# Probability buffers as fixed tiles taken in turn, with the writes of one buffer declared ordered, in a one-core adaLN attention and Mish MLP block

## The chip, the cores and the metric

The kernel runs on one core of a Trainium2 chip, alone. The metric is the device time of one launch in microseconds (us), the median over several runs. Before the change it is 1747.98 us, the median of three runs (1747.57, 1747.98 and 1752.33).

The core has five engines that each take their instructions strictly in order: PE (TensorE, matrix products), ACT (ScalarE, exponentials and copies), DVE (VectorE, maxima and sums), POOL (GpSimd) and SP (which issues the transfers). They meet only through semaphores: an instruction may wait until a counter of another engine, or of its own, has reached a value.

## The reference, cut to what matters

```python
B, S, D = 1, 2048, 512
H = 32; Dh = D // H                 # 32 heads of 16
scale = Dh ** -0.5
scores = jnp.einsum("bhqd,bhkd->bhqk", q, k) * scale
p = _softmax(scores, axis=-1)
o = jnp.einsum("bhqk,bhkd->bhqd", p, v)
...
x = x + ga * _A_ref(h, A_wqkv, A_wo)                  # h: layer norm of x, scaled and shifted
x = x + gb * _B_ref(h, B_w1, B_b1, B_w2)              # dense, Mish, dense; F = 1792
```

All inputs and the output are 32-bit floats. The softmax runs over 2048 keys for each of 2048 queries and 32 heads, so 32 x 2048 x 2048 exponentials are taken; these are the "probabilities".

## The kernel before, in words

**Tiling.** The queries are cut into 4 blocks of 512 and the heads into 8 groups of 4, which gives 32 iterations `n`. An iteration goes over the 2048 keys in 16 chunks of 128, so there are 512 steps `t` (`t = 16 n + chunk`), recorded one after the other by `step`. In each step four score products are made (`score`, the matmul of line 507: 64 rows of the array, 512 queries wide), each is exponentiated by ACT (line 510, `nc.scalar.activation(pr, p_, AF.Exp, ...)`) into a probability buffer `pr`, and four products of probabilities with values follow two steps later (`pv`, line 525, output `bk`, input `vg` and `pr`). Beside that, each step makes four products for the row maxima of a later iteration (`max_tile`, line 470), which DVE reduces (line 472), and a part of other work: projections, output projection and MLP of the query block before (line 132).

**Buffers.** Scores and maxima share a ring of six PSUM banks (`ring`). A score product can start when the exponential or the maximum that used its bank six turns ago has been read out. The probabilities go into SBUF tiles of 128 x 512 floats: four tags `p0` to `p3`, one for each head of the group, with 3 buffers for the heads of the lower half of the rows (`s = 0`) and 4 for the upper half (`s = 1`), 14 buffers in all. The pool hands them out: `ap.tile([P, TB], F32, tag=f"p{2 * j + s}", name="pr", bufs=3 + s)`. The pool `ap` is made with `reuse_waits="tile"`. The tail of the kernel takes eight tiles of the same tags for the last query block (`y` and `xn`).

**Order.** Nothing is reordered by a scheduler: the kernel is recorded under `manual_schedule`, so each engine's order is that of the code. What the recording layer adds are the waits. An exponential into a buffer that was used before must not start before the values' product has read the old contents (a wait on PE, which it needs for its scores anyway) and, in the layer's view, must also come after the older exponential that wrote that buffer (a wait of ACT on its own counter). Where one instruction has to wait for two counters, the first wait stands in a separate EVENT_SEMAPHORE instruction ahead of it in the same queue.

Of the kernel before, what the change touches and what calls it, by code (L numbers as in the profile page):

```python
# [8 lines left out]
F32 = mybir.dt.float32  # L9
# [9 lines left out]
def adaln_block(ctx: ExitStack, tc: tile.TileContext, x, wqkv, wo, w1, b1, w2, c, w_mod, out):  # L19
    nc = tc.nc  # L20
    P = 128
    S, D = x.shape[1], x.shape[2]
# [5 lines left out]
    TB = 512  # L28
# [4 lines left out]
    T = 16 * NIT  # L33
# [66 lines left out]
    def layernorm(pool, xt, xn, eng="v"):  # L100
        st = pool.tile([P, 6], F32, tag="ln_st", name="ln_st", bufs=4)
        mv = pool.tile([P, 2], F32, tag="ln_mv", name="ln_mv", bufs=4)
        rs = pool.tile([P, 2], F32, tag="ln_rs", name="ln_rs", bufs=4)
        nc.vector.bn_stats(out=st, in_=xt)
        nc.vector.bn_aggr(out=mv, in_=st)
        nc.gpsimd.tensor_scalar(rs[:, 0:1], mv[:, 1:2], 1.0, EPS, op0=ALU.mult, op1=ALU.add)
        nc.gpsimd.tensor_tensor(rs[:, 1:2], rs[:, 0:1], nhalf, op=ALU.pow)
        eng = nc.vector if eng == "v" else nc.gpsimd
        return lambda: eng.tensor_scalar(xn, xt, mv[:, 0:1], rs[:, 1:2], op0=ALU.subtract, op1=ALU.mult)
# [28 lines left out]
    def pe_run():  # L138
        while pe_queue:
            mm_go(pe_queue.pop(0))  # L140
# [6 lines left out]
    def ring(w=1):  # L147
        if w == 2 and ring_at[0] % 2:
            ring_at[0] += 1
        b = ring_at[0] % NRING  # L150
        ring_at[0] += w
        return ring_t[:, b, :] if w == 1 else ring_t[:, b:b + 2, :]

    def bank(tag="ms"):
        return ring() if tag == "ring" else ps.tile([P, TB], F32, tag=tag, name="bk", bufs=1)
# [153 lines left out]
    with ExitStack() as es:  # L309
# [28 lines left out]
        e = lp.tile([P, DK], F32, name="sil_e")  # L338
# [39 lines left out]
        pr, pm = [], ring()[:, :2 * DK].rearrange("p (i k) -> p i k", k=DK)  # L378
# [72 lines left out]
    ap = ctx.enter_context(tc.tile_pool(name="ap", bufs=1, reuse_waits="tile"))  # L451
# [46 lines left out]
                        mt[o:o + 8, :].bitcast(F32))  # L498
        at(2 * (16 * n + 16 - PRO) + 3, put)

    pts = {}

    def score(n, j, s, kc):
        def product():
            kt, qt = ka[(2 * n + j) % NR], qa[(2 * n + j) % NR]
            p_ = ring()
            nc.tensor.matmul(p_, kt[64 * s:64 * s + 64, kc * P:(kc + 1) * P], qt[64 * s:64 * s + 64, :],  # L507
                             start=True, stop=True)
            pr = ap.tile([P, TB], F32, tag=f"p{2 * j + s}", name="pr", bufs=3 + s)
            e = nc.scalar.activation(pr, p_, AF.Exp, scale=SCALE)  # L510
            pts[16 * n + kc, 2 * j + s] = pr
            return e
        return product
# [67 lines left out]
    def evac_last(ps_):  # L581

        ot, od, rb = mst["last"]
        oh, ol = o_hl[NB - 1]
        r = slice(64, P)
        dn, on = ps_
        pick = mst["pick"]
        nc.tensor.matmul(dn[r, :], pick[:, 1, :], ot, start=True, stop=True)
        nc.tensor.matmul(on[r, :], pick[:, 0, :], ot, start=True, stop=True)
        nc.vector.reciprocal(rb[r], dn[r, :])  # L590
        nc.vector.tensor_mul(od[r], on[r, :], rb[r])
        hi_copy("v", oh[r, DK - 1, :], od[r])
        lo_sub("v", ol[r, DK - 1, :], od[r], oh[r, DK - 1, :])
# [67 lines left out]
    def load_w2(f):  # L661
        return load_split("w2", NA, w2scr[f])
# [14 lines left out]
    def put_h(hh, hl, acc, k, tail):  # L677
        hf = mst["p"].tile([P, TB], F32, tag="ee", name="hf2", bufs=2)
        nc.scalar.activation(hf, acc, AF.Identity, scale=modc[:, 3, k:k + 1], bias=modc[:, 2, k:k + 1])
        hi_copy("p", hh[:, k, :], hf)  # L680
        lo_sub("v" if tail else "p", hl[:, k, :], hf, hh[:, k, :])

    def up_mms(acc, w, hh, hl):
        mm3(acc, [w1v(w, 0, k) for k in range(DK)], [w1v(w, 1, k) for k in range(DK)],
            [hh[:, k, :] for k in range(DK)], [hl[:, k, :] for k in range(DK)], "b")

    def mish(f, acc, tail):

        mp = mst["p"]
# [176 lines left out]
    def w1_tail(f):  # L866
        i, j = divmod(f % 8, 2)
        return load_w1(f) if i == 1 else half_tile(ka[(1, 0, 2, 3)[i]], j, w1scr[f])
# [7 lines left out]
    def tail():  # L876

        oh, ol = o_hl[last]
        mp = mst["p"]
        y, xn = [], []  # L880
        for v in (y, xn):
            for i in range(4):
                v.append(ap.tile([P, D], F32, tag=f"p{i}", name="y", bufs=3 + i % 2))
        for i in range(4):
            r = 4 * last + i
            nc.sync.dma_start(y[i], x[r * P:(r + 1) * P, :])
        for f in range(4, 8):
            w1s[f] = w1_tail(f)
        accs4 = [bank("ms"), bank("acc")] + [None, None]

        def wo_mms(i, ks):
            s = slice(i * P, (i + 1) * P)
            seq = [(l, r, k) for l, r in ((oh, 0), (oh, 1), (ol, 0)) for k in ks]
            for j, (l, r, k) in enumerate(seq):
                nc.tensor.matmul(accs4[i], l[:, k, s], wos[k][:, r, :], start=(k == 0 and j == 0),
                                 stop=(k == 3 and j == 2))

        wo_mms(0, (0, 1, 2))
        t = ring(2)
        evac_last([t[:, i, :] for i in range(2)])  # L900
        wo_mms(1, (0, 1, 2))
        for i in (2, 3):
            accs4[i] = bank("ring")
            wo_mms(i, (0, 1, 2))
        app = []
        for i in range(4):
            wo_mms(i, (3,))
            nc.vector.tensor_add(y[i], accs4[i], y[i])
            app.append(layernorm(mp, y[i], xn[i]))
            if i:  # L910
                app[i - 1]()
        app[3]()

        def held(js):
            t = ring(2)
            fins = []
            for i, j in enumerate(js):
                fins.append(mst["held"](j, t[:, i, :]))
                pe_run()
            return fins  # L920

        for js in ((0, 1), (2, 3)):
            for f in held(js):
                f(None)
        hh, hl = [mp.tile([P, DK, TB], F32R, tag=f"h2_{v}", name="h2", bufs=1) for v in range(2)]
        fins = held((4,))
        accs = [bank(("ring", "ms", "ring", "acc")[k]) for k in range(DK)]
        for k in range(DK):
            for i in range(4):
                nc.tensor.transpose(accs[k][:, i * P:(i + 1) * P], xn[i][:, k * P:(k + 1) * P], ident)  # L930
        for k in range(DK):
            put_h(hh, hl, accs[k], k, True)
        fins += held((5, 6))
        for f in fins:
            f(None)
        for f in held((7,)):
            f(None)
        for f in range(6):
            w2s[f] = load_w2(f)
        po = [ring(2) for _ in range(2)]  # L940
        free2 = ring(2)
        act, stages = {}, {}
        LAG = 4
        for u in range(FT + LAG):
            if u < FT:
                acc = free2[:, u // 2 % 2, :] if u % 2 else bank(("ms", "acc")[u // 2 % 2])
                up_mms(acc, w1s.pop(u), hh, hl)
                pe_run()
                if u + 8 < FT:
                    w1s[u + 8] = w1_tail(u + 8)  # L950
                act[u], stages[u] = mish(u, acc, True)
            for d, ss in ((2, (4, 5)), (1, (2, 3)), (0, (0, 1))):
                if 0 <= u - d < FT:
                    for q in ss:
                        stages[u - d][q]()
            f = u - LAG
            if f >= 0:
                a_h, a_l = act.pop(f)
                w = w2s.pop(f)
                for i in range(4):  # L960
                    s = slice(i * P, (i + 1) * P)
                    for j, (l, r) in enumerate(((a_h, 0), (a_h, 1), (a_l, 0))):
                        nc.tensor.matmul(po[i // 2][:, i % 2, :], l[:, s], w[:, r, :], start=(f == 0 and j == 0),  # L963
                                         stop=(f == FT - 1 and j == 2))
                    if f == FT - 1 and i % 2:
                        for q in (i - 1, i):
                            nc.vector.tensor_add(y[q], po[q // 2][:, q % 2, :], y[q])
                            r = 4 * last + q
                            nc.sync.dma_start(out[r * P:(r + 1) * P, :], y[q])
                if f + 6 < FT:  # L970
                    w2s[f + 6] = load_w2(f + 6)
# [276 lines left out]
```

## Time and profile before

| what | value |
|---|---|
| median of three runs | 1747.98 us (1747.57 to 1752.33) |
| profiled execution, its span from first to last instruction | 1752.7 us |
| PE / DVE / ACT / POOL busy in it | 1711.7 / 1464.5 / 1341.6 / 751.4 us |
| exponentials (line 510) | 2048, 604 ns mean |
| EVENT_SEMAPHORE instructions of line 510 on ACT | 553 |
| mean granted TensorE clock | 0.996 |

The profiled execution's span is 4.7 us above the median of the runs and close to the slowest of the three; only its span is known, and what lies around it is not recorded. Busy time is the time in which at least one instruction of the engine runs. Neighbouring instructions of ACT, DVE and PE overlap, so an engine can begin a new one before the last has ended: durations are longer than the distance from one start to the next. "Idle before" a row is the engine's gap and who ended it. Records of matmuls have modelled ends, so a PE that is busy by the record may still be held up.

### The profile page before, as it was taken

How to read it: one execution, taken by the hardware profiler on the slowest of the kernel's cores; microseconds unless marked ns; L12 is line 12 of the kernel's file. 1: busy time of each engine (PE TensorE's matmuls, PEld its weight loads, DVE VectorE, ACT ScalarE, POOL GpSimd, SP SyncE). 2: the span in 40 equal slices, each digit the busy share in tenths (PEclk: the TensorE clock that was granted, in tenths of full speed). 3: DMA queues.
4: the chain of work that ended last, by engine and by line, in shares of the span. 5: the costliest groups of instructions: out<-in, count | busy, mean ns of one | idle time of the engine just before them, and what ended most of it. 6: DMA issues, size and time to landing. Idle time of an engine off the chain costs nothing.

```text
span 1752.7 us, 33365 instructions
## 1 busy us (share of the span) xinstructions
PE 1711.7 (98%) x12230; PEld 954.7 (54%) x12230; DVE 1464.5 (84%) x2464; ACT 1341.6 (77%) x2565; POOL 751.4 (43%) x740
## 2 busy tenths in 40 slices
PE   7999999999999999999999999999999999999999
PEld 5755665555435455555455455555455455554687
DVE  6888888887888998888989898888989899891477
ACT  6247777777777898797877898797877799897464
POOL 5145224656303275263312276173412267162852
PEclk9999999999999999999999999999999999999999
DMA  7676467777662342432435443442435434422451
GB/s 236 181 234 196 119 170 208 236 238 220 207 196 63 110 117 71 143 101 67 104 108 144 126 114 80 121 120 52 120 82 158 113 102 102 126 79 71 153 228 61
DMA packets 113996, 240.05 MB, mean 137 GB/s; under 512 B 24048, under 2 KB 49648, under 8 KB 107784
## 3 DMA queue, kind: packets, MB, share of 16 engines
q1 hardware_dynamic: 113832, 237.92, 47.5%
q8 instruction: 96, 1.57, 0.4%
q14 instruction: 68, 0.56, 0.1%
HBM read 179.95 MB, written 51.44 MB: 132 GB/s over the span
## 4 chain that ended last, share of the span: by engine, by line
PE 80%; DMA 6%; DVE 4%; ACT 3%; POOL 3%; issue 2%; SPq 2%; POOLq 0%; ACTq 0%; DVEq 0%
PE bk L525 26%; PE ring L470 20%; PE ring L507 18%; PE bk L132 11%; DVE mx L472 3%; ACT pr L510 2%; DMA qscr<-ql 2%; PE ring L126 2%; PE ring L963 1%; PE bk L126 1%; DMA kscr<-ql 1%; DMA wr<-in_A_wqkv 1%; DMA w2scr<-hl 1%; DMA vg<-vscr 0%; SPq L317 0%
## 5 line engine op out<-in xcount | busy, mean ns | idle before, releaser
L472 DVE TENSOR_REDUCE mx<-ring 128x1 f32<-128x512 f32 x2048 | 1273.9, 683 | 176.9 <-PE ring L470 145.1
L510 ACT ACTIVATE pr<-ring 128x512 f32<-128x512 f32 x2048 | 1080.7, 604 | 274.7 <-PE bk L132 148.2
L470 PE MATMUL ring<-ka,qa 64*128 64x512 f32 x2048 | 847.6, 431 | 1.1 <-DVE mx L472 0.2
L507 PE MATMUL ring<-qa,ka 64*128 64x512 f32 x2048 | 737.4, 401 | 11.8 <-ACT pr L510 10.5
L470 PEld LDWEIGHTS ring<-ka,qa 64*128 64x128 f32 x2048 | 364.8, 184 | 398.3 <-DVE mx L472 321.8
L525 PE MATMUL bk<-pr,vg 128*32 128x512 f32 x4096 | 547.0, 606 | 0.0
L507 PEld LDWEIGHTS ring<-qa,ka 64*128 64x128 f32 x2048 | 372.5, 185 | 119.9 <-ACT pr L510 64.3
L132 PE MATMUL bk<-h,w 64*128 64x512 f32 x996 | 275.9, 409 | 1.4 <-ACT pr L510 1.2
L132 PEld LDWEIGHTS bk<-h,w 64*128 64x128 f32 x996 | 171.1, 184 | 17.5 <-ACT pr L510 7.7
L132 PE MATMUL bk<-w,a_h 64*128 64x512 f32 x576 | 167.2, 414 | 0.3
L525 PEld LDWEIGHTS bk<-pr,vg 128*32 128x32 f32 x4096 | 80.7, 108 | 138.6 <-issue 133.4
L830 POOL TENSOR_TENSOR y<-yd,y 128x512 f32<-128x512 f32 x40 | 51.9, 1303 | 214.2 <-ACT yd L829 193.6
L711 POOL TENSOR_TENSOR hb<-hb,ee 128x512 f32<-128x512 f32 x42 | 53.9, 1284 | 178.2 <-DVE ee L710 178.2
L132 PEld LDWEIGHTS bk<-w,a_h 64*128 64x128 f32 x576 | 96.4, 184 | 12.0 <-ACT pr L510 6.7
L724 POOL TENSOR_TENSOR qq<-ee,rr 128x512 f32<-128x512 f32 x42 | 54.4, 1295 | 75.3 <-ACT rr L717 72.7
L132 PE MATMUL bk<-w,o_hl 64*128 64x512 f32 x288 | 80.6, 411 | 1.6 <-POOL o_hl L95 1.0
L132 PE MATMUL bk<-w,a_l 64*128 64x512 f32 x288 | 76.9, 390 | 0.0
L98 POOL TENSOR_TENSOR a_l<-hb,a_h 128x512 fp32r<-128x512 f32 x53 | 72.3, 1363 | 4.4
L132 PE MATMUL bk<-h_h,wl 64*128 64x512 f32 x168 | 57.2, 421 | 0.0
L710 DVE SCALAR_TENSOR_TENSOR ee<-ee 128x512 f32<-128x512 f32 x56 | 39.8, 711 | 19.3 <-ACT ee L707 19.3
L727 POOL TENSOR_TENSOR hb<-hb,rr 128x512 f32<-128x512 f32 x42 | 54.4, 1296 | 3.3
L132 PEld LDWEIGHTS bk<-w,a_l 64*128 64x128 f32 x288 | 53.0, 184 | 4.8
(186 smaller groups left out, 1735.8 us busy)
## 6 DMA issues: line engine op xcount, KB each, us to landing
ka<-kscr SPq DMA_DIRECT2D x124, 384.0 KB
w<-w2scr SPq DMA_DIRECT2D x56, 512.0 KB
w<-w1scr SPq DMA_DIRECT2D x46, 512.0 KB
vg<-vscr SPq DMA_DIRECT2D x32, 552.0 KB
qa<-qscr SPq DMA_DIRECT2D x124, 100.0 KB
kscr<-qh SPq DMA_DIRECT2D x16, 512.0 KB
qscr<-qh SPq DMA_DIRECT2D x32, 256.0 KB
hl<-in_B_w SPq DMA_DIRECT2D x28, 256.0 KB
```

The costliest lines, as they stand in the source:

```text
L98: (nc.gpsimd if eng == "p" else nc.vector).tensor_sub(lo, src, hi.bitcast(F32))
L126: nc.tensor.matmul(acc, l, r, start=start, stop=stop)
L132: i = nc.tensor.matmul(acc, l[64 * g:64 * g + 64], r[64 * g:64 * g + 64], start=start, stop=stop)
L470: nc.tensor.matmul(pm, qt[64 * s:64 * s + 64, qs * P:(qs + 1) * P], kt[64 * s:64 * s + 64, kb * TB:(kb + 1) * TB], start=True, stop=True)
L472: nc.vector.tensor_reduce(out=mxs[n][:, s, 4 * j + qs, kb:kb + 1], in_=pm, op=ALU.max, axis=AX.X)
L507: nc.tensor.matmul(p_, kt[64 * s:64 * s + 64, kc * P:(kc + 1) * P], qt[64 * s:64 * s + 64, :], start=True, stop=True)
L510: e = nc.scalar.activation(pr, p_, AF.Exp, scale=SCALE)
L525: nc.tensor.matmul(accs[n][32 * h:32 * h + 32, :], vgs[n][:, o:o + 32], pts.pop((t, h)), start=(kc == 0), stop=(kc == 15))
L711: (nc.vector if tail else nc.gpsimd).tensor_mul(hb, hb, ee)
L724: nc.gpsimd.tensor_mul(qq, ee, rr)
L727: nc.gpsimd.tensor_mul(hb, hb, rr)
L830: nc.gpsimd.tensor_add(y[i], yd, y[i])
```

## The change

The pool is no longer asked for a probability buffer in each `score`. At the first use of a head `h = 2 j + s` of the group its 3 or 4 buffers are made as tiles of their own and kept in `prs[h]`; after that `score` takes buffer `(16 n + kc) % (3 + s)`. For the second and every later exponential into a buffer, the layer is told by `declare_no_dep` that it need not order the two writes by a wait, since the values' product between them reads the buffer. The tail takes its eight tiles out of the same fixed buffers. The whole difference:

```diff
-    pts = {}
+    pts, prs, exps = {}, {}, {}
 
     def score(n, j, s, kc):
         def product():
...
             nc.tensor.matmul(p_, kt[64 * s:64 * s + 64, kc * P:(kc + 1) * P], qt[64 * s:64 * s + 64, :],
                              start=True, stop=True)
-            pr = ap.tile([P, TB], F32, tag=f"p{2 * j + s}", name="pr", bufs=3 + s)
+            h, b = 2 * j + s, (16 * n + kc) % (3 + s)
+            if h not in prs:
+                prs[h] = [ap.tile([P, TB], F32, name=f"pr{h}_{i}") for i in range(3 + s)]
+            pr = prs[h][b]
             e = nc.scalar.activation(pr, p_, AF.Exp, scale=SCALE)
+            if (h, b) in exps:
+                tc.declare_no_dep(e.ins, exps[h, b].ins, reason="the values' product between them reads it")
+            exps[h, b] = e
             pts[16 * n + kc, 2 * j + s] = pr
             return e
         return product
...
-        y, xn = [], []
-        for v in (y, xn):
-            for i in range(4):
-                v.append(ap.tile([P, D], F32, tag=f"p{i}", name="y", bufs=3 + i % 2))
+        y, xn = ([prs[i][(T + v) % (3 + i % 2)] for i in range(4)] for v in range(2))
```

In the built programs PE, DVE, POOL and SP have the same instructions in the same order with the same waits as before; only line numbers and the names of the buffers differ. The 14 buffers lie at the same addresses, handed out in another phase. On ACT the order is the same too, and the waits differ. Counting the rows of ACT's order, 549 of the 2048 exponentials wait on ACT's own counter before and none does now; 160 other instructions of ACT do so before and 190 now.

ACT's order at the end of one iteration, before. `pr<-ring` is an exponential, `x3` three alike, `ot<-bk` the copy of an iteration's result out of PSUM; the row of three starts at 486.30 us of the span, the copy at 499.60 us:

```order
L510 ACTIVATE pr<-ring 128x512 [waits PE_49] x36
L510 ACTIVATE pr<-ring 128x512 [waits PE_49,Activation_49] x3
L510 ACTIVATE pr<-ring 128x512 [waits PE_49] x5
L510 ACTIVATE pr<-ring 128x512 [waits DVE_49,PE_49]
L510 ACTIVATE pr<-ring 128x512 [waits PE_49] x11
```

The same place with the change, from the last exponential ahead of those three to the one after the next four (each buffer now has a name of its own, `pr_1` being the second buffer of a head, so no two neighbouring rows are alike):

```order
L513 ACTIVATE pr_1_1158<-ring 128x512 [waits PE_49]
L513 ACTIVATE pr_1_1176<-ring 128x512 [waits PE_49]
L513 ACTIVATE pr_1_1183<-ring 128x512 [waits PE_49]
L513 ACTIVATE pr_2_1177<-ring 128x512 [waits PE_49]
L513 ACTIVATE pr_2_1184<-ring 128x512 [waits PE_49]
L513 ACTIVATE pr_2_1151<-ring 128x512 [waits PE_49]
```

Nothing moved; the three exponentials (the second to fourth row) lost the wait on ACT's own counter and with it the separate wait instruction, and the wait on PE stays and stands on the exponential itself. Elsewhere on ACT the copy of an iteration's result shows the other side, with the change:

```order
L545 COPY ot<-bk 128x512 [waits DMAHW2_49,DMAHW1_49,DMAHW3_49,DMAHW0_49,DMAHW7_49,PE_49,Activation_49]
L545 COPY ot<-bk 128x512 [waits DMAHW1_49,DMAHW4_49,PE_49,Activation_49]
```

These copies waited for transfers and PE before; 7 of the 32 now wait for an earlier ACT instruction as well.

## Prediction

> **What bounds the kernel now.** I read the page first (busy times, then the chain of waits), then stretches of the span, then the table of waits, and last single steps in the timeline.
>
> ```profile
> PE 1711.7 (98%) x12230; PEld 954.7 (54%) x12230; DVE 1464.5 (84%) x2464; ACT 1341.6 (77%) x2565; POOL 751.4 (43%) x740
> PE 80%; DMA 6%; DVE 4%; ACT 3%; POOL 3%; issue 2%; SPq 2%; POOLq 0%; ACTq 0%; DVEq 0%
> PE bk L525 26%; PE ring L470 20%; PE ring L507 18%; PE bk L132 11%; DVE mx L472 3%; ACT pr L510 2%; DMA qscr<-ql 2%; PE ring L126 2%; PE ring L963 1%; PE bk L126 1%; DMA kscr<-ql 1%; DMA wr<-in_A_wqkv 1%; DMA w2scr<-hl 1%; DMA vg<-vscr 0%; SPq L317 0%
> ```
>
> PE carries four fifths of the chain; the exponentials (ACT pr L510), where all of the change lies, carry 2%, and ACT's queue (ACTq, its separate wait instructions) rounds to nothing. Two stretches of the span say the same, a long middle one and the last steps, in which the maxima have ended:
>
> ```profile
> core 0: us, PE busy (x) PEld busy (x) DVE busy (x) ACT busy (x) POOL busy (x), PEclk, DMA share, GB/s
> 690.00:1090.00 400.00, 397.08 (x2945) 209.51 (x2941) 355.27 (x605) 333.46 (x646) 163.35 (x156) 1.00 0.42 110
> 1560.00:1620.00 60.00, 59.61 (x429) 29.41 (x425) 22.27 (x40) 49.68 (x97) 22.97 (x21) 1.00 0.21 66
> ```
>
> PE has under 3 us without work in 400 (400.00 - 397.08), at a granted clock of 1.00, and ACT is busy for 333 of 400. What remains to be asked is how often PE stands still for an exponential:
>
> ```profile
> ACT pr L510 <- PE bk L132: 148.2, 228, 1.6
> ACT pr L510 <- PE ring L507: 92.6, 149, 2.5
> ACT pr L510 <- PE ring L470: 30.2, 44, 1.1
> PEld ring L507 <- ACT pr L510: 64.3, 96, 2.6
> PE ring L507 <- ACT pr L510: 10.5, 36, 2.1
> PE bk L132 <- ACT pr L510: 1.2, 2, 0.6
> ```
>
> Exponentials found ACT idle and waited for PE 421 times (228 + 149 + 44). The other way round, PE stood idle for an exponential only 38 times, 11.7 us in all (10.5 + 1.2); the 96 weight loads that waited were mostly hidden behind running matmuls.
>
> Where this happens is seen in one step of the chain (start, length, what):
>
> ```profile
> 488.61 0.42 PE ring L507
> 489.03 0.05 PE ring L470
> 489.08 0.59 ACT pr L510
> 489.67 0.04 issue
> 489.72 0.50 PE ring L507
> ```
>
> The step's first exponential frees the bank that its fourth score needs. Here, in a step without projection or MLP work, the start of an exponential does count.
>
> **The change part by part.** Names, fixed tiles and the tail's reuse of them move no instruction and leave PE, DVE, POOL and SP as they were, so they cost nothing; no cover is needed for that. The wait that protects a buffer from being overwritten too early, the one on PE, stays in every row. It cannot become later by the fixed turn either: the product that read the old contents was issued in the step before at the latest, ahead of the score that the exponential reads, and PE is in order.
>
> What goes is ACT's wait for its own older exponential, in 549 of 2048 rows of its order (27%), and with it the separate instruction that held the wait on PE. That older exponential was long done, the same buffer being taken three or four chunks later, so the wait itself took no time. The instruction ahead could take time:
>
> ```profile
> L510 ACTq EVENT_SEMAPHORE  x553: 17/17/1687, 111.4 to 1616.7; - x185
> L510 ACTq EVENT_SEMAPHORE  x1: 17/17/17, 486.2 to 486.2; - x1
> 486.30 2.06 ACT L510 ACTIVATE pr<-ring 128x512 f32<-128x512 f32 x4 [0.99 <-PE ring L470]
> 489.07 2.07 ACT L510 ACTIVATE pr<-ring 128x512 f32<-128x512 f32 x4 [0.70 <-PE ring L470]
> 485.70 0.50 PE L507 MATMUL ring<-qa,ka 64*128 64x512 f32 x1
> 488.54 0.49 PE L507 MATMUL ring<-qa,ka 64*128 64x512 f32 x1
> ```
>
> The second row is the wait instruction of the four exponentials that start at 486.30; those at 489.07 have none. With it, ACT starts 0.10 us after its score has ended (486.30 - 485.70 - 0.50), without it 0.04 us (489.07 - 488.54 - 0.49). So a run of exponentials that finds ACT idle starts **0.06 us** earlier without the separate instruction. Behind a running exponential it costs nothing: three of the four at 486.30 had one, none at 489.07, and four take 2.06 against 2.07 us.
>
> How many of these 0.06 us lie on the path? Three bounds.
> Above: all starts from idle, 421 x 27% = 113, times 0.06 = 6.8 us, if every one of them were on the path.
> Below: the pieces of ACT's queue that the chain itself names with a length. Around the last steps it has, for instance,
>
> ```profile
> 1599.47 0.02 PE ring L507
> 1599.49 0.02 issue
> 1599.52 0.02 ACTq L510
> 1599.53 0.04 issue
> 1599.58 0.19 ACT pr L510
> ```
>
> and one more in that stretch, the rest rounding to 0% of the span: 2 x 0.06 = 0.1 us.
> Between: the chain's 2.1% of the span in exponentials, 36.8 us, are about 61 of them at 0.60 us (the rows are below). If 27% start behind a wait instruction, that is 16 x 0.06 = **1.0 us**. PE's own idle time for exponentials gives about as much: 38 x 27% x 0.06 = 0.6 us. I take 1.0, since idle time of PE is hidden where a neighbouring matmul still runs, and the chain counts those cases too.
>
> ```profile
> by line: PE bk L525 26.0%; PE ring L470 19.6%; PE ring L507 18.2%; PE bk L132 10.6%; DVE mx L472 2.5%; issue 2.2%; ACT pr L510 2.1%; DMA qscr<-ql 2.0%; PE ring L126 1.8%; PE ring L963 1.5%; PE bk L126 1.3%; DMA kscr<-ql 0.7%; DMA wr<-in_A_w
> L510 ACT ACTIVATE pr<-ring x2048: 577/600/693, 110.2 to 1634.0; 128x512 f32<-128x512 f32 x187
> L539 ACTq EVENT_SEMAPHORE  x87: 17/38/38, 212.2 to 1638.1; - x87
> 1596.37 0.59 ACT ot L539
> ```
>
> Added are 30 waits of other ACT instructions for an older ACT instruction (160 rows before, 190 now), 7 of them on the copies `ot`, behind which the next step's four exponentials queue, and behind those its scores. Their transfers already needed wait instructions of their own (87 for 32 copies), and the older exponential is far behind. If each brought 0.06 us to the path it would be 1.8 us; the chain names one such copy around the last steps, so I take 0.1. What is late next: PE again, which has no more than the next score or maximum ready.
>
> Sum: -1.0 + 0.1 = -0.9 us, 1751.8 for the profiled span of 1752.7. That span is 4.7 us above the median and near the slowest run; taken off the median, **1747.1 us**, bounded by 1741.2 (-6.8) and 1749.8 (+1.8).
>
> **The rivals.** *All starts count (faster).* The recorded ends of matmuls are modelled, so PE may be held up more often than its 11.7 us of idle time show; then the whole 6.8 us come back: 1741.2. Against it stands that a gain in one step needs PE to be waiting there, and in the middle stretch it has 3 us without work in 400.
>
> *A wait instruction costs the queue its time wherever it stands (faster).* Then 549 x 0.06 = 33 us go: 1715. The equal 2.06 and 2.07 us speak against it. This is what a rule in the Trainium skill would give (page "Advanced Engine Details and Errata", section on miscellaneous facts, network and communication): reading a semaphore from the sequencer takes 50 to 100 ns on trn2. By that price 549 of them would be an estimated 27 to 55 us; the trace agrees with it only for a start from idle, where 60 ns are seen, and not in the queue.
>
> *The freed exponentials get slower (slower).* ACT and DVE read PSUM and ACT writes SBUF beside PE. Exponentials that start earlier, into buffers that are handed out in another phase, would take longer wherever accesses now coincide. The place is the step shown above, in which the fourth score waits for the first exponential; there are about 61 such on the chain. From (5.2 + 0.9) / 61 = 0.10 us more each, that is 0.70 instead of 0.60 us, it makes the kernel slower by 0.3% (5.2 us) net of the gain: 1753.2. Against it: among 2048 exponentials with all kinds of neighbours half take 577 to 600 ns, and the 14 buffers stay where they are.
>
> *The change does nothing on the chip.* The wait instructions are gone in the built program, but all might be hidden: 1748.0, within the same bounds as my forecast.
>
> **How the numbers follow.** A difference of 0.3%, 5.2 us, is about what a measurement of this kernel can tell from no change (the three runs span 4.8 us). My forecast of 1747.1 gets 0.75, no effect at all 0.07, all starts 0.09, the full price in the queue 0.03, slower exponentials 0.06. The first two are within 0.3%: 0.82. Faster by more: 0.12. Slower by more: 0.06. The range reaches from 1742.5, most of the way to the full gain, to 1751.0, which holds the bound of the added waits (1749.8) and a median drawn one run closer to the slowest.
>
> **What would show it.** Right: the EVENT_SEMAPHORE row of line 510 all but vanishes on ACT (553 now); runs of exponentials that found ACT idle start 0.04 us after their score everywhere; the mean of an exponential stays near 604 ns; PE's 38 waits and 11.7 us stay nearly as they are; the chain's share of exponentials stays at 2%. Wrong: a step like the one at 488.61 that gets shorter by more than 0.06 us, four queued exponentials that take less than 2.06 us, a mean of the exponentials near 700 ns, or new waits in front of `ot` that the chain names often.

## The result and the profile after

The changed kernel takes 1744.15 us, the median of nine runs (1738.31 to 1745.45), against 1747.98 us (nine runs, 1746.46 to 1752.33). The ratio is 0.9972 with a 95% interval of 0.9961 to 0.9984: faster by 0.28%, 3.8 us by the medians. The forecast was 1747.1 us in a range of 1742.5 to 1751.0. Side and bound (within 0.3%) held; the gain is about four times the 0.9 us that the sum gave. The nine runs of before include the three that were known ahead of the prediction.

The page after, with the lines that answer to those of before (busy times, chain by engine and by line):

```profile
span 1740.6 us, 32834 instructions
PE 1699.3 (98%) x12230; PEld 942.2 (54%) x12230; DVE 1464.0 (84%) x2464; ACT 1341.4 (77%) x2565; POOL 752.8 (43%) x740
PE 80%; DMA 6%; DVE 4%; ACT 4%; POOL 3%; SPq 2%; issue 1%; POOLq 0%; ACTq 0%; DVEq 0%
PE bk L531 26%; PE ring L470 19%; PE ring L507 18%; PE bk L132 11%; ACT pr L513 2%; DVE mx L472 2%; PE ring L126 2%; DMA qscr<-ql 1%; PE ring L966 1%; DMA w2scr<-hl 1%; PE bk L126 1%; DMA kscr<-ql 1%; DMA xt<-in_A_x 1%; DMA hl<-in_B_w 1%; DMA wm<-in_w_mod 0%
```

It has 531 instructions fewer (33365 before), all of them separate wait instructions of ACT. In the chain's shares nothing has moved by more than about 1%. The exponentials' own rows (duration min/median/max, first and last start) and PE's two waits for them:

```profile
L513 ACT ACTIVATE pr<-ring x2048: 585/599/692, 105.0 to 1621.8; 128x512 f32<-128x512 f32 x187
L513 ACTq EVENT_SEMAPHORE  x6: 17/17/38, 106.2 to 1574.2; - x6
```

```profile
PE ring L507 <- ACT pr L513: 9.9, 36, 1.5
PE bk L132 <- ACT pr L513: 1.2, 2, 0.6
```

553 wait instructions became 6, the exponentials take as long as before, and PE's idle time for them fell by 0.6 us (from 11.7 to 11.1), no more. By this view the gain would indeed be about 0.6 us.

**The profiled spans mislead.** 1752.7 and 1740.6 us differ by 12.1 us, three times what the medians differ by. The mean granted TensorE clock of the two executions is part of it:

```profile
core 0: 1752.7 us, clock 0.996
```

```profile
core 0: 1740.6 us, clock 0.999
```

0.003 of 1750 us is 5.2 us of PE's time, an estimate that takes PE for the bound throughout. Another part lies before 575 us, where the chain still runs through transfers whose landing varies from one execution to the next: the first exponential already starts 5.2 us earlier with the change (at 105.0 instead of 110.2 us). What can be compared is the stretch behind that, with the clock at 1.00 in both. There the distance between two groups of values' products, those of `t` = 201 and `t` = 481, is free of such luck. Before (start, length, engine, line, what):

```profile
724.13 1.06 PE L525 MATMUL bk<-pr,vg 128*32 128x512 f32 x8
...
1556.19 1.06 PE L525 MATMUL bk<-pr,vg 128*32 128x512 f32 x8
```

After:

```profile
715.20 1.07 PE L531 MATMUL bk<-pr,vg 128*32 128x512 f32 x8
...
1544.19 1.07 PE L531 MATMUL bk<-pr,vg 128*32 128x512 f32 x8
```

280 steps take 832.06 us before and 828.99 us after: 3.07 us less, without a transfer on the path. Compared step by step over the whole kernel (distance from one group of values' products to the next, 510 steps), 94 steps became 0.04 to 0.08 us shorter, 5.5 us in sum, and 14 became as much longer, 0.7 us. So the 0.06 us of the prediction are there, but in some 90 steps and not in 16. How could the profile of before not show them? One such step, before (a choice of its rows):

```profile
881.45 1.07 PE L525 MATMUL bk<-pr,vg 128*32 128x512 f32 x8
882.78 0.39 PE L507 MATMUL ring<-qa,ka 64*128 64x512 f32 x1
883.27 1.58 ACT L510 ACTIVATE pr<-ring 128x512 f32<-128x512 f32 x3 [0.83 <-PE bk L132]
883.92 0.18 PEld L470 LDWEIGHTS ring<-ka,qa 64*128 64x128 f32 x1
883.94 0.48 PE L470 MATMUL ring<-ka,qa 64*128 64x512 f32 x1
883.94 0.39 PE L507 MATMUL ring<-qa,ka 64*128 64x512 f32 x1
884.35 0.64 PE L525 MATMUL bk<-pr,vg 128*32 128x512 f32 x4
```

The same step after:

```profile
872.19 1.06 PE L531 MATMUL bk<-pr,vg 128*32 128x512 f32 x8
873.52 0.39 PE L507 MATMUL ring<-qa,ka 64*128 64x512 f32 x1
873.94 1.57 ACT L513 ACTIVATE pr<-ring 128x512 f32<-128x512 f32 x3 [0.76 <-PE bk L132]
874.59 0.18 PEld L470 LDWEIGHTS ring<-ka,qa 64*128 64x128 f32 x1
874.67 0.39 PE L507 MATMUL ring<-qa,ka 64*128 64x512 f32 x1
874.68 0.41 PE L470 MATMUL ring<-ka,qa 64*128 64x512 f32 x1
875.02 0.64 PE L531 MATMUL bk<-pr,vg 128*32 128x512 f32 x4
```

The exponential starts 0.10 us after its score ended before (883.27 - 882.78 - 0.39) and 0.03 us after with the change. 0.65 us after its start, in both, PE loads the weights of the step's last maximum product, whose bank it has freed (883.92 and 874.59). This half of the array waits; the other half goes on with a score, so PE is never idle by the record. The delayed product's record starts on time (883.94, 2.49 us into the step, as with the change) and is longer, 0.48 instead of 0.41 us. The values' products need the whole array and come 0.07 us later: the step lasts 2.90 us before and 2.83 us after. In the table of PE's waits nothing of this appears, and the chain goes from the values' products to the matmul just before them, past ACT.

The step is typical. In 91 of the 94 steps the last weight load of line 470 comes 0.04 to 0.07 us earlier in the step than before, and in 90 of these 91, in either trace, it starts 0.65 us (within 0.015) after the start of an exponential; the other three steps have no maximum products. On the page the loss stands in the busy time of line 470, where it looks like work:

```profile
L470 PE MATMUL ring<-ka,qa 64*128 64x512 f32 x2048 | 847.6, 431 | 1.1 <-DVE mx L472 0.2
L470 PE MATMUL ring<-ka,qa 64*128 64x512 f32 x2048 | 840.3, 427 | 1.1 <-DVE mx L472 0.2
```

The first row is before, the second after. Summed over the records of line 470 it is 7.8 us less, 5.3 of them in the 94 steps. The scores of line 507, matmuls of the same shape, lost 1.0 us, and nothing in the 94 steps.

That is also why PE's busy time was no bound: in the stretch from 690 to 1090 us PE is busy for 397.08 us before and 397.12 us after, with 2945 matmuls in the one and 2956 in the other. The row of after:

```profile
690.00:1090.00 400.00, 397.12 (x2956) 208.40 (x2952) 356.32 (x607) 333.89 (x646) 163.74 (x156) 1.00 0.42 110
```

These 400 us do not hold quite the same work in both. The 280 steps do, and it is plainer there: 6116 matmuls in either trace, for which PE is busy 826.44 us before and 823.47 after, and without work for 5.62 and 5.52 us. Of the 3.07 us gained, 2.97 were on record as busy time.

### The profile page after: what moved, and what is told of

Same layout as the page of the kernel before. It is cut to its first block, busy times and chain, and to the rows that moved or that the text cites. A ratio compares the mean times of both kernels' runs of the same rounds, so it can differ in the third digit from the quotient of the medians.

```text
span 1740.6 us, 32834 instructions
## 1 busy us (share of the span) xinstructions
PE 1699.3 (98%) x12230; PEld 942.2 (54%) x12230; DVE 1464.0 (84%) x2464; ACT 1341.4 (77%) x2565; POOL 752.8 (43%) x740
## 4 chain that ended last, share of the span: by engine, by line
PE 80%; DMA 6%; DVE 4%; ACT 4%; POOL 3%; SPq 2%; issue 1%; POOLq 0%; ACTq 0%; DVEq 0%
PE bk L531 26%; PE ring L470 19%; PE ring L507 18%; PE bk L132 11%; ACT pr L513 2%; DVE mx L472 2%; PE ring L126 2%; DMA qscr<-ql 1%; PE ring L966 1%; DMA w2scr<-hl 1%; PE bk L126 1%; DMA kscr<-ql 1%; DMA xt<-in_A_x 1%; DMA hl<-in_B_w 1%; DMA wm<-in_w_mod 0%
## 5 line engine op out<-in xcount | busy, mean ns | idle before, releaser
L507 PE MATMUL ring<-qa,ka 64*128 64x512 f32 x2048 | 736.4, 400 | 11.7 <-ACT pr L513 9.9
L732 POOL TENSOR_TENSOR rr<-rr,qq 128x512 f32<-128x512 f32 x42 | 54.2, 1290 | 3.5
```

Source lines behind the costliest of these rows:

```text
L732: nc.gpsimd.tensor_mul(rr, rr, qq)
```

## The experiments

All start from the changed kernel. Beside each measured ratio stands the distance of the 280 steps (832.06 before, 828.99 after), which tells tenths of a us that the whole time does not. The declaration alone, on the pool's tiles of the kernel before, builds to the same program as before, with all 549 waits in ACT's order, and was therefore not run.

**The change again.**

> The changed kernel once more, timed beside the others. Three theories are compared here and in the runs beside it. Start theory: the gain is the 0.06 us by which a run of exponentials that finds ACT idle starts earlier when the wait on PE no longer stands in a separate instruction; PE feels it in some 90 of the 510 steps. Buffer theory: the fixed tiles and their other phase bring the gain. Count theory: each of the 531 instructions that ACT's queue lost cost it about the same, 3.8 us / 531 = 7 ns, wherever it stood. All three expect about 1744 us here, 0.997 of the kernel before.

Measured: 1744.76 us, ratio 0.9969 (0.9957 to 0.9981); 829.02 us for the 280 steps. The gain repeats.

**Fixed tiles without the declaration.**

```diff
-            if (h, b) in exps:
-                tc.declare_no_dep(e.ins, exps[h, b].ins, reason="the values' product between them reads it")
```

> The change without its declaration: fixed tiles taken in turn, and the 549 waits of ACT on its own counter stay, with their separate instructions. Start theory and count theory: as slow as the kernel before, 1748 us, ratio 1.000. Buffer theory: as fast as the change, 1744 us, ratio 0.997.

Measured: 1749.7 us, ratio 1.0001 (0.9991 to 1.0012); 831.88 us. The wait instructions are all back:

```profile
L513 ACTq EVENT_SEMAPHORE  x553: 17/17/1690, 107.8 to 1613.0; - x185
```

The buffers' new phase and the fixed turn bring nothing clear of the noise. The buffer theory falls.

**The wait given back, by place.** Four kernels give ACT's wait for its own earlier work back to a chosen part of the exponentials; the edit is the same, and only the list `EXTRA` (one bit for each of the 2048 exponentials) differs. The work that is waited for is long done in each.

```diff
+    made, EXTRA = [], int("...", 16)
...
+            if len(made) >= 6 and EXTRA >> len(made) & 1:
+                tc.add_manual_dep(e.ins, made[-6].ins.name,
+                                  mybir.DependencyInfo(mybir.DependencyClass.Sync, mybir.DependencyReason.DATA),
+                                  reason="the sixth last exponential")
+            made.append(e)
```

At exponentials that find ACT idle:

> The changed kernel, with a wait for the sixth last exponential given back to 649 exponentials that found ACT idle in the profile of the change (about 540 of them get a separate instruction that holds the wait on PE; the rest is covered by an earlier wait). Start theory: about 190 starts behind such an instruction cost some 4.8 us in the kernel before, 0.025 us each on the end, so 540 cost about 13.6 us: 1758 us, ratio 1.005, and clearly slower than the kernel before. Count theory: 522 instructions more than the change, as many as before: 1748 us, ratio 1.000. Buffer theory: 1744 us.

Measured: 1756.37 us, ratio 1.0044 (1.0031 to 1.0056); 836.13 us. Its row and two groups of products:

```profile
L514 ACTq EVENT_SEMAPHORE  x544: 17/17/1727, 110.4 to 1630.6; - x182
```

```profile
720.33 1.06 PE L537 MATMUL bk<-pr,vg 128*32 128x512 f32 x8
...
1556.46 1.07 PE L537 MATMUL bk<-pr,vg 128*32 128x512 f32 x8
```

It has as many wait instructions as the kernel before (544 against 553) and is slower than it by 0.44%: 231 steps are 0.04 to 0.08 us longer than with the change, 13.5 us in sum. By the medians it lost 11.6 us (1756.37 - 1744.76) where 13.6 were expected. The count theory, which expected no difference to the kernel before, falls.

At exponentials that queue behind another:

> The changed kernel, with the same wait given back to 788 exponentials whose score had been ready for at least 0.15 us when they started, since another exponential was running (some 410 get the separate instruction). Start theory: none of them starts later, 1744 us, ratio 0.997. Count theory: 395 instructions at 7 ns, 2.8 us: 1747 us, ratio 0.9994. Buffer theory: 1744 us.

Measured: 1745.31 us, ratio 0.9972 (0.9961 to 0.9984); 829.07 us, 0.05 from the second run of the change, with 411 more wait instructions:

```profile
L514 ACTq EVENT_SEMAPHORE  x417: 17/17/227, 107.3 to 1624.3; - x139
```

A wait instruction in the queue behind running work costs nothing that is seen here; one of the 94 steps became longer by 0.04 us or more.

In the 94 steps that became shorter, and at the rest of the 549:

> The changed kernel, with the wait given back to 252 of the 549 exponentials that had it before: those in the 94 steps that the two traces show to have become 0.04 to 0.08 us shorter with the change. Start theory: the whole gain goes, 94 x 0.06 = 5.6 us at most: ratio to the kernel before 1.000, 1749 us. Count theory: 252 / 531 of the gain goes: ratio 0.9985. Chain theory (the prediction's 1.0 us, of which these steps would have no special share): ratio 0.998.

Measured: 1746.92 us against 1747.58 of the kernel before in that session, ratio 0.9998 (0.9987 to 1.0009); 830.95 us.

> The changed kernel, with the wait given back to the other 297 of the 549. Start theory: nothing goes, ratio 0.997, 1744.5 us. Count theory: 297 / 531 of the gain goes: ratio 0.9987. Chain theory: ratio 0.998.

Measured: 1746.22 us, ratio 0.9984 (0.9974 to 0.9994); 829.09 us.

The steps separate the two: the 252 waits on the path give back 1.96 of the 3.07 us, the other 297 give back 0.10. Of the 94 steps, 88 became longer by 0.04 us or more with the first, 5.3 us over the whole kernel, and three with the second. The chain theory, by which the places are alike, does not hold, nor does the count theory.

The 280 steps show two thirds of the loss and the whole time all of it, and the steps tell why. Of the 3.07 us, 2.61 were gained in those of the 94 that lie in this stretch, and the waits on the path take 2.55 of them away. Three other steps are 0.25 to 0.33 us shorter with the change (one of them followed by a step 0.21 us longer), 0.7 us in sum; neither half of the waits takes that away, all 549 together (the fixed tiles alone) do, and why they need both was not looked into. The rest is spread over changes of less than 0.04 us a step.

The whole times alone would not separate the two halves: the medians are 0.7 us apart, and the intervals overlap. The second kernel's ratio is 0.0012 to 0.0015 above that of the change (0.9972 and 0.9969), where the steps show nearly nothing; the intervals of 0.9974 to 0.9994 and of 0.9957 to 0.9981 overlap. In its one profiled execution, the time that it has more than the change (4.4 us from 100 to 1650 us) lies between 300 and 575 us, 4.1 us. There the granted clock is at 0.50 for 6.8 us from 520.8 us, and the three steps around it take 3.1 us more than with the change. The kernel with waits at queued exponentials has 6.0 us more in the same stretch in its own profiled execution (1749.32 us), though its median is that of the change. So this looks like chance and not like these waits; that the median is 1746.22 us stays without an explanation.

## Why the prediction was right, and which term was mis-sized

**What goes and what stays.** Right: only ACT's wait instructions went, PE's order and waits stayed (38 waits, 11.1 us), and the exponentials' mean stayed at 604 ns.

**0.06 us for each start from idle, nothing in the queue.** Right, as the four kernels with waits given back show. In the traces, exponentials that found ACT idle with a wait instruction in front start 0.06 us later after their release than those without (medians of 82 and 23 ns), and with the change none of 420 has one. The rule of the Trainium skill ("Advanced Engine Details and Errata", miscellaneous facts on network and communication: 50 to 100 ns to read a semaphore from the sequencer) fits the 60 ns of a start from idle. As a price of each instruction it fails: 411 of them at queued exponentials cost 0.05 us in 280 steps.

**How many of them lie on the path: this term was mis-sized.** The sum took 16 starts, 1.0 us, from the chain's share of exponentials, with 0.6 us from PE's idle time as a check. Some 94 steps gained, 5.5 us, less 0.7 us in the steps that became longer. By the number of starts the upper bound, 113 and 6.8 us, was nearer; the 27% in it were low as well, since in the trace of before a wait instruction stands in front of 140 of the 422 exponentials that found ACT idle (33%). Both of the prediction's smaller estimates counted only waits at which all of PE stands. The wait that mattered held one half of the array, at a weight load, while the other half worked, so it was in no idle time and in no link of the chain. The prediction saw such loads wait (96 times for a score) and set them aside as mostly hidden behind running matmuls. The sentence that a gain needs PE to be waiting, and that PE has 3 us without work in 400, was the false step; in the 280 steps PE's time without work fell by 0.1 us, and its busy time, for the same matmuls, by 2.97 us.

**What was luck.** The measured 3.8 us lie about midway between the 0.9 us of the sum and the 6.8 us of the rival in which all starts count. The range holds them because it was drawn most of the way to that rival, not because the sum was good, and the bound of 0.3% was met narrowly: the repeat gives 0.9969.

**The added waits, 0.1 us.** No separate run; the profile names five waits of `ot` for an exponential, 1.1 us on ACT in all:

```profile
  ACT ot L545: 1.1, 5
```

The copies do not stand out in the chain (four pieces, 2.2 us, against five and 2.8 us before).

**The rivals.** That all starts count has the mechanism nearest to what was seen, with PE held up more than its idle time shows; its 6.8 us are above the 3.8 us measured. Slower exponentials did not come (604 ns), nor the full price in the queue (1715 us). No effect at all (1748.0 us) is excluded by the interval and by the repeat. The fixed turn alone does nothing, as measured; the declaration is what took the waits away, and it needed tiles whose successive writes can be named.

**The signs the prediction named.** The wait instructions of line 510 vanished and the exponentials stayed as they were, as named; four queued ones take 2.07 us after as before (the median). The prediction looked for shorter steps among those without projection or MLP work, like the one at 488.61, where the exponential is a link of the chain; all of the 94 steps that became shorter carry matmuls of line 132 (projections, output projection or MLP) beside the scores, like the one shown above, and none of the 55 steps without such work is among them.

## What to carry to other kernels

Where an in-order engine has to wait for two counters and one of the waits is in a separate instruction, remove the other wait, if the order is already implied. (Whether it is enough to put the late wait on the instruction itself and the early one in front, no run here shows.) It pays only where the engine stands idle for it: behind running work the wait instruction cost nothing here. Whether such a delay reaches the end is not read from the idle time of a tiled TensorE: look for a weight load that waits for the late engine while the other half works, and for matmuls of one shape that are recorded longer than their neighbours. To see a gain of a few us, compare the same step of two traces rather than the spans: here spans differed by 12.1 us, the medians by 3.8, and 280 steps by 3.07 with a repeat within 0.03 us (829.02 against 828.99).

## What the runs showed of the hardware that was not expected

A stretch of 829 us repeats to 0.03 us between two executions of the same program (828.99 and 829.02), and to 0.10 us in the kernels whose added waits are off the path (829.07 and 829.09), though the whole times of these four executions are 1742.38, 1742.00, 1749.32 and 1748.23 us. Their differences come from outside that stretch: from the transfers in the first third, and from the granted clock. In all eight profiles the clock is at 1.00 but for pieces of 3.4 or 6.8 us at 0.50 before 530 us of the span (before the change at 98.5, 409.1 and 525.2 us, after it at 358.9 alone) and one at its very end. At half speed the 13.6 us of the one and the 3.4 us of the other cost at most 6.8 and 1.7 us, an estimate that agrees with the 5.2 us above. Over the runs of the change the clock's mean is between 0.996 and 0.999.
